# Eighteen loads of one input move from SyncE's DMA queue to ScalarE's, every engine keeping its order

## The chip, the cores and the metric

The kernel runs on one core of one Trainium2 chip. The metric is the device time of one execution in microseconds. Before the change it was 199.9 us, the median of three runs (199.68 to 200.76). About half a per cent, 1.0 us here, is what a measurement of this kernel can tell from no change.

## The reference, cut to what matters

Two stages. The first is a recurrence over 768 time steps for 4 batches and 8 heads with head size 40; its output, laid out as 4 x 768 x 320, is the input `x` of the second, a mixer over tokens and channels.

```python
for t in range(S):                                    # per batch and head, state is 40 x 40
    y[t]  = r[t] @ state
    Sa    = state @ a[t]
    state = state * w[t][:, None] - outer(Sa, b[t]) + outer(v[t], k[t])
...
theta = x @ w_theta
zr, zi = x * cos(theta), x * sin(theta)
u = x + w_tok_r @ zr + w_tok_i @ zi                   # over the 768 tokens
out = u + max(u @ w_ch, 0)
```

All inputs and the output are 32-bit floats.

## The kernel before, in words

The 768 steps of each of the 4 batches are cut into 6 chunks of 128, so there are 24 tiles, numbered 0 to 23, each with 128 steps in the partitions and 8 heads x 40 values in a row. Within a tile the recurrence is written as matrix products, so a tile is a long chain over all engines. A tile's decay factors come first: ScalarE takes the logarithm of `w` (tile `lw`), TensorE sums it over time, ScalarE takes exponentials (`ex`, and `we` for the sum without the step itself). GpSimd then multiplies: `kb` is `k` or `b` by `ex`, and `ah` is `a` by `we` (function `product`, line 456, the only reader of the input `a`; `DVE` does it for tiles 0 and 1). TensorE transposes `ah` (lines 404 and 408), ScalarE or VectorE copies the transposed piece out of PSUM as `aT`, and TensorE multiplies `aT` with the transposed `kb` into score matrices (line 603), which VectorE or ScalarE masks (lines 612 and 614). More products follow for the state and the read-out. Once the six tiles of a batch are read out, its mixer stage (the products of line 910 on TensorE, sines on ScalarE, products with `x` on GpSimd) is worked in between the tiles of the next batch; that of the last batch ends the kernel.

The order of all the work is written out by hand. Each step is recorded as an `Op` by `add`, with its engine and with what it reads and writes; `Plan.order` then emits the steps in the order of the list `ORDER`, a permutation of 1602 numbers. An engine executes its own instructions strictly in that order, and waits at each for what it needs. The list `HOMES` gives each result its PSUM bank, `PICK` names the steps that go to their second engine.

Every input load of the recurrence is issued by SyncE, whose work in the kernel is issuing DMAs and waiting to be allowed to: `loads(i)` records for tile `i` the loads of `w`, `k`, `b`, `a` and from tile 8 on `v` (line 436), and for every second tile two loads of `r` (and of the early `v`) for two tiles at once (line 448). A load of 160 KB goes in rows of 40 floats, 160 bytes each. Its buffer is one of a ring: 5 buffers for `a` (`raw_a`, named `raw_a_68` to `raw_a_72` in the built program), 4 each for `w` and for `k` with `b` (`raw_kb`). A load may be issued once the buffer's last reader is done. Besides, the DMAs of SyncE and ScalarE share eight semaphores in turn, so each waits until the DMA eight places earlier in `ORDER` has landed. GpSimd issues the loads of the mixer's weights (lines 961 and 989), and SyncE the stores of the result and, late in the program, eleven DMA transposes. ScalarE issues one DMA, half of the last store (line 938).

Of the kernel before, what the change touches and what calls it, by code (L numbers as in the profile page):

```python
# [19 lines left out]
FROM_POOL = 4  # L20
EXCLUSIVE = 7
# [198 lines left out]
def kernel(  # L220
# [14 lines left out]
    nc = tc.nc  # L235
# [19 lines left out]
    raw_a = sb("raw_a", [128, H, D], FP32, NA)  # L255
# [820 lines left out]
```

## Time and profile before

| | |
|---|---|
| median of the runs | 199.9 us (199.68 to 200.76) |
| span of the profiled execution, first to last instruction | 195.9 us |
| time of the profiled execution itself | not among the three, so the median stands for it: 4.0 us lie outside the span |
| TensorE matmuls busy | 184.3 us, 94% |
| VectorE busy | 163.3 us, 83% |
| ScalarE busy | 150.6 us, 77% |
| GpSimd busy | 145.1 us, 74% |
| queue of SyncE's DMAs | 29.19 MB, packets for 76.6% of 16 engines' span |
| queue of GpSimd's DMAs | 2.97 MB, 9.3% |
| queue of ScalarE's DMAs | 0.08 MB, 0.1% |

In the profile's lines `PE` is TensorE's matmuls, `PEld` its weight loads, `DVE` VectorE, `ACT` ScalarE, `POOL` GpSimd. `SPq` and `ACTq` are the instruction sequencers of SyncE and ScalarE: waiting for semaphores and issuing DMAs, during which the arithmetic unit of ScalarE is not counted as busy. `L456` is line 456 of the kernel. A DMA has three times: its issue begins, the issue takes a while on the sequencer, and the data land later.

### The profile page before, as it was taken

The page shows a single profiled execution, that of the slowest core. Times are in us where ns is not written, and L with a number is a line of the kernel's source. Part 1 is how long each engine was busy: PE and PEld are TensorE (multiplying, and loading weights), DVE is VectorE, ACT ScalarE, POOL GpSimd, SP SyncE. Part 2 cuts the span into 40 slices and gives each one's busy share as a digit, 9 for nine tenths or more (in the row PEclk, how much of TensorE's full clock was granted, in tenths as well). Part 3 has the DMA queues.
Part 4 walks back from the last instruction along what each step waited for, and adds up shares of the span by engine and source line. Part 5 has one row for each costly group of instructions (what it writes and reads, how often), then busy time and mean ns, then how long its engine had stood idle before and what let it go on. Part 6 is the DMA issues. An engine that isn't in the chain of part 4 may idle for free.

```text
span 195.9 us, 8473 instructions
## 1 busy us (share of the span) xinstructions
PE 184.3 (94%) x3516; PEld 145.4 (74%) x3516; DVE 163.3 (83%) x260; ACT 150.6 (77%) x336; POOL 145.1 (74%) x211
## 2 busy tenths in 40 slices
PE   7889899999997999999899999999999999999992
PEld 6767687887786778887577787887788768767661
DVE  5378799999998999898897999999999938664453
ACT  3575879799997997999689599979999867575111
POOL 8367466579969999696699959868879997469100
PEclk9999999999999999999999999999999999999998
DMA  5999897999999999979999997789899977535055
GB/s 118 217 205 182 148 214 157 174 171 206 216 183 166 197 180 185 225 122 200 179 183 158 166 200 129 164 147 180 161 178 203 168 172 102 128 136 74 32 197 172
DMA packets 134646, 32.78 MB, mean 167 GB/s; under 512 B 124816, under 2 KB 134608, under 8 KB 134608
## 3 DMA queue, kind: packets, MB, share of 16 engines
q1 hardware_dynamic: 131680, 29.19, 76.6%
q0 software_dynamic: 2784, 2.97, 9.3%
q8 instruction: 27, 0.44, 0.9%
q10 hardware_dynamic: 144, 0.08, 0.1%
q14 instruction: 11, 0.09, 0.1%
HBM read 29.54 MB, written 3.93 MB: 171 GB/s over the span
## 4 chain that ended last, share of the span: by engine, by line
PE 61%; DMA 12%; POOL 9%; ACT 6%; DVE 4%; SPq 4%; issue 2%; ACTq 0%; DVEq 0%; POOLq 0%
PE banks L910 16%; PE banks L603 9%; PE banks L404 8%; PE banks L792 5%; DMA raw_a<-in_a_dram 4%; DMA raw_kb<-in_k_dram 4%; SPq L436 3%; PE banks L408 3%; DMA uT<-up 2%; PE banks L569 2%; PE banks L663 2%; POOL kb L456 2%; PE banks L686 2%; PE banks L802 2%; DMA raw_v<-in_v_dram 2%
## 5 line engine op out<-in xcount | busy, mean ns | idle before, releaser
L456 POOL TENSOR_TENSOR kb<-raw_kb,ex 128x320 bf16<-128x320 f32 x46 | 37.1, 814 | 8.0 <-DMA raw_kb<-in_k_dram 3.0
L910 PE MATMUL banks<-zr,wtok_r 128*128 128x320 bf16 x144 | 41.0, 300 | 0.2
L910 PE MATMUL banks<-zi,wtok_i 128*128 128x320 bf16 x144 | 40.8, 299 | 0.1
L456 POOL TENSOR_TENSOR ah<-raw_a,we 128x320 bf16<-128x320 f32 x22 | 19.0, 865 | 12.9 <-ACT we L506 4.7
L612 DVE TENSOR_TENSOR lamu<-banks,mask_p 128x1024 bf16<-128x1024 f32 x22 | 26.8, 1219 | 1.5 <-PE banks L603 0.8
L612 DVE TENSOR_TENSOR psi<-banks,mask_p 128x1024 bf16<-128x1024 f32 x22 | 26.8, 1219 | 0.8 <-PE banks L603 0.7
L612 DVE TENSOR_TENSOR phi<-banks,mask_n 128x1024 bf16<-128x1024 f32 x18 | 21.9, 1216 | 1.6 <-POOL r L462 1.3
L612 DVE TENSOR_TENSOR lamv<-banks,mask_p 128x1024 bf16<-128x1024 f32 x17 | 20.7, 1219 | 1.6 <-PE banks L603 1.0
L894 POOL TENSOR_TENSOR zi<-cs,xp 128x320 bf16<-128x320 f32 x22 | 17.2, 791 | 2.0 <-ACT cs L879 1.2
L910 PEld LDWEIGHTS <-wtok_r 128*128 128x128 bf16 x144 | 14.0, 97 | 5.6 <-issue 0.3
L603 PE MATMUL banks<-aT,kbT 64*128 64x128 bf16 x384 | 17.2, 217 | 0.9 <-DVE kbT L426 0.3
L894 POOL TENSOR_TENSOR zr<-cs,xp 128x320 bf16<-128x320 f32 x22 | 17.4, 802 | 0.1
L910 PEld LDWEIGHTS <-wtok_i 128*128 128x128 bf16 x144 | 14.0, 98 | 3.8 <-issue 0.3
L829 PE MATMUL banks<-kb,lamv 128*128 128x40 bf16 x192 | 14.9, 180 | 0.0
L831 PE MATMUL banks<-kb,lamu 128*128 128x40 bf16 x192 | 14.8, 179 | 0.0
L603 PEld LDWEIGHTS <-kbT 64*128 64x128 bf16 x384 | 11.8, 94 | 3.7 <-ACT kbT L422 1.1
L829 PEld LDWEIGHTS <-lamv 128*128 128x128 bf16 x192 | 13.2, 96 | 0.4
L916 DVE TENSOR_TENSOR up<-banks,xp 128x320 bf16<-128x320 f32 x22 | 10.6, 485 | 3.1 <-PE banks L910 2.9
L831 PEld LDWEIGHTS <-lamu 128*128 128x128 bf16 x192 | 13.0, 96 | 0.0
L472 ACT ACTIVATE lw<-raw_w 128x320 bf16<-128x320 f32 x24 | 11.5, 477 | 1.5 <-DMA raw_w<-in_w_dram 1.3
L496 ACT ACTIVATE ex<-banks 128x328 f32<-128x328 f32 (+1 forms) x24 | 10.8, 450 | 2.2 <-PE banks L491 1.1
L822 PE MATMUL banks<-gd,rT 128*128 128x80 bf16 x80 | 12.2, 197 | 0.0
(202 smaller groups left out, 583.0 us busy)
## 6 DMA issues: line engine op xcount, KB each, us to landing
raw_w<-in_w_dram SPq DMA_DIRECT2D x24, 160.0 KB, 4.3
raw_v<-in_v_dram SPq DMA_DIRECT2D x24, 160.0 KB, 3.7
raw_a<-in_a_dram SPq DMA_DIRECT2D x24, 160.0 KB, 3.9
raw_kb<-in_k_dram SPq DMA_DIRECT2D x24, 160.0 KB, 4.2
raw_kb<-in_b_dram SPq DMA_DIRECT2D x24, 160.0 KB, 4.2
raw_r<-in_r_dram SPq DMA_DIRECT2D x24, 160.0 KB, 3.8
out_dram<-oo SPq DMA_DIRECT2D x9, 160.0 KB, 2.6
wrow_i<-in_moe_w_tok_i_dram POOLq DMA_DIRECT2D x6, 192.0 KB, 5.3
```

The source lines that it names most:

```text
L404: nc.tensor.transpose(out=t[:, m * 128:m * 128 + 128], in_=src, identity=ident)
L456: pool = ("POOL", lambda: nc.gpsimd.tensor_tensor(out=dst, in0=in0, in1=in1, op=ALU.mult))
L472: add("ACT", "ln", i, lambda: nc.scalar.activation(out=paired(lw)[:, :, :, 0:D], in_=paired(raw_w[s4]), func=AF.Ln), 473, [("raw_w", s4)], ...
L496: got = add("ACT", "exp", i, lambda: nc.scalar.activation(out=ex[:, :, 0:D] if no_total else ex.rearrange("p h x -> p (h x)"), in_=sums(ps ...
L603: nc.tensor.matmul(t[:, q, g, :], lhsT=lhs[g][rows(q)], rhs=rhs[g][rows(q)], start=True, stop=True)
L612: add("DVE", kindm, i, lambda: nc.vector.tensor_tensor(out=flat, in0=whole(), in1=mask.to_broadcast([128, 2 * G, 128]), op=ALU.mult), 1217 ...
L822: nc.tensor.matmul(t[:, g * 80:g * 80 + 80], lhsT=by_two(rT)[g], rhs=gd[:, 2 * g:2 * g + 2, :], start=True, stop=False, skip_group_check=True)
L829: nc.tensor.matmul(o, lhsT=lamv[:, p, g, :], rhs=kb[:, 0, h, 0:D], start=first, stop=False, skip_group_check=True)
L831: nc.tensor.matmul(o, lhsT=lamu[:, p, g, :], rhs=kb[:, 1, h, 0:D], start=False, stop=True, skip_group_check=True)
L894: pool = ("POOL", lambda: nc.gpsimd.tensor_tensor(out=dst, in0=in0, in1=in1, op=ALU.mult))
L910: nc.tensor.matmul(acc(), lhsT=wtok[nm][j][:, s], rhs=zs[c][:, s], start=n == 0 and c == 0, stop=n == NT - 1 and c == 1)
L916: add("DVE", "uadd", q, lambda: nc.vector.tensor_tensor(out=u, in0=acc(), in1=x, op=ALU.add), 488, [pk, x_key(q)], [u_key(q)], at="row")
```

## The change

The loads of `a` of tiles 6 to 23, eighteen of them, are recorded for ScalarE and issued with `nc.scalar.dma_start` in place of `nc.sync.dma_start`. Nothing else is loaded, computed or stored in another way, and the buffers are the same. `ORDER` is written anew: a moved load stands behind the ScalarE instruction that was running when SyncE issued that load in the kernel before, and the other instructions stand on every engine as they stood.

```diff
+SECOND = 6
...
 ORDER = [
-    0, 7, 3, 6, 1, 20, 2, 21, 8, 23, 24, 4, 27, 32, 9, 30, 22, 33, 31, 25, 5, 34, 26, 12, 28,
+    0, 7, 3, 6, 1, 20, 2, 21, 23, 8, 24, 27, 30, 4, 32, 31, 9, 22, 33, 5, 25, 12, 26, 34, 69,
...
     def loads(i):
         for key, dst, src in load(i):
-            add("SP", "l" + key[0][4:], i,
-                lambda dst=dst, src=src: nc.sync.dma_start(out=dst, in_=src),
-                600, [], [key], work=1030)
+            other = key[0] == "raw_a" and i >= SECOND
+            add("ACT" if other else "SP", "l" + key[0][4:], i,
+                lambda dst=dst, src=src, q=nc.scalar if other else nc.sync: q.dma_start(
+                    out=dst, in_=src), 600, [], [key], work=1030)
```

In the changed file the lines below the new constant have a number that is one higher, and those below the load two higher.

SyncE's program about the load of `a` for tile 13, some 86 us into the profiled execution; `raw_v_77` and the like are buffers of the inputs that follow the letter.

```order
L436 DMA raw_v_77<-in_v_dram 128x8x40
L448 DMA raw_r_80<-in_r_dram 128x1x320
L436 DMA raw_a_71<-in_a_dram 128x8x40
L436 DMA raw_v_78<-in_v_dram 128x8x40
L436 DMA raw_kb_75<-in_k_dram 128x8x40
```

The same place of SyncE's program after the change.

```order
L438 DMA raw_v_77<-in_v_dram 128x8x40
L450 DMA raw_r_80<-in_r_dram 128x1x320
L438 DMA raw_v_78<-in_v_dram 128x8x40
L438 DMA raw_kb_75<-in_k_dram 128x8x40
L438 DMA raw_kb_75<-in_b_dram 128x8x40
```

The load has left the row, and the load of `v` moves up behind that of `r`. ScalarE's program at the same time, before: `gd` is the state for the read-out, `aT` the transposed `ah`, `we` the exponential that `ah` needs, `psi` a score matrix.

```order
L718 CAST gd_209<-banks 128x320
L718 CAST gd_208<-banks 128x320
L422 COPY aT_184<-banks 128x256
L514 ACTIVATE we_179<-sx_183 128x320
L614 ACTIVATE psi_198<-banks 128x1024
```

The same place of ScalarE's program after the change.

```order
L720 CAST gd_209<-banks 128x320
L720 CAST gd_208<-banks 128x320
L423 COPY aT_184<-banks 128x256
L438 DMA raw_a_71<-in_a_dram 128x8x40
L516 ACTIVATE we_179<-sx_183 128x320
```

The load now stands between two computing instructions, ahead of the exponential `we`, and everything behind it on ScalarE comes one place later.

188 rows, old and new, of the table ORDER are left out of this document.

## The prediction

> **What bounds the kernel now.** I read the page first: busy shares, the slices, and the chain of work that ended last.
>
> ```profile
> span 195.9 us, 8473 instructions
> PE 184.3 (94%) x3516; PEld 145.4 (74%) x3516; DVE 163.3 (83%) x260; ACT 150.6 (77%) x336; POOL 145.1 (74%) x211
> DMA  5999897999999999979999997789899977535055
> PE 61%; DMA 12%; POOL 9%; ACT 6%; DVE 4%; SPq 4%; issue 2%; ACTq 0%; DVEq 0%; POOLq 0%
> ```
>
> TensorE's matmuls are busy for 94% of the span and are 61% of the chain. So a microsecond saved elsewhere counts only where TensorE stood still for it, and one lost counts only where TensorE then stands still. The DMA digits are at 9 nearly all the way to the last fifth: the transfers run close to what is moved at all, but they are 12% of the chain, not the bound. Next I asked where the chain passes through a load.
>
> ```profile
> 45.14 0.38 POOL wrow_i L989
> ...
> 48.22 7.07 DMA raw_kb<-in_k_dram
> 55.36 0.58 POOL kb L456
> ...
> 86.11 8.33 DMA raw_a<-in_a_dram
> 94.58 0.88 POOL ah L456
> ```
>
> Two loads in the steady part land late, at 55 us a load of `k` and at 94 us a load of `a`, each while GpSimd's own loads are under way (the first row is one of their issues). Then the list of waits, for what that lateness costs.
>
> ```profile
> POOL ah L456 <- DMA raw_a<-in_a_dram: 3.4, 1, 3.4
> ...
> POOL kb L456 <- DMA raw_kb<-in_k_dram: 3.0, 2, 1.8
> ...
> PEld L408 <- POOL ah L456: 1.4, 2, 1.1
> ```
>
> GpSimd waits 3.4 us once for `a`, but TensorE waits for `ah` only 1.4 us in two places together (total, times, longest). This 1.4 us is the most that earlier loads of `a` and `k` can be worth at these two places. The rest of GpSimd's waiting never reaches TensorE.
>
> Then ScalarE, which takes over the issues, in stretches of 20 us (stretch, length, busy us and instructions, TensorE's granted clock, DMA share, GB/s).
>
> ```profile
> 20.00:40.00 20.00, 16.72 (x44) 1.00 0.89 175
> 40.00:60.00 20.00, 18.70 (x45) 1.00 1.04 192
> 60.00:80.00 20.00, 18.00 (x41) 1.00 1.04 183
> 80.00:100.00 20.00, 17.58 (x36) 1.00 1.00 175
> 100.00:120.00 20.00, 16.74 (x39) 1.00 0.93 170
> 120.00:140.00 20.00, 18.38 (x44) 1.00 0.89 166
> 140.00:160.00 20.00, 18.92 (x41) 1.00 0.93 181
> ```
>
> It is idle 3.28, 1.30, 2.00, 2.42, 3.26, 1.62 and 1.08 us in them. That is the room for new work, and it is small in three of the seven.
>
> **The change, part by part.** What it removes: eighteen issues from SyncE. The row of the tile and SyncE's timeline say how long such an issue takes (start, length).
>
> ```profile
> L436 SPq DMA_DIRECT2D raw_a<-in_a_dram x24: 575/630/1815, 2.0 to 148.2; - x24
> ...
> DMA to landing us min/median/max: 3.0/3.9/8.7
> ```
>
> ```profile
> 40.04 1.81 SPq L436 DMA_DIRECT2D raw_a<-in_a_dram  x1
> 41.95 0.69 SPq L436 DMA_DIRECT2D raw_kb<-in_k_dram  x1
> ...
> 51.27 0.66 SPq L436 DMA_DIRECT2D raw_a<-in_a_dram  x1
> ...
> 56.34 0.63 SPq L436 DMA_DIRECT2D raw_a<-in_a_dram  x1
> 65.00 0.58 SPq L436 DMA_DIRECT2D raw_a<-in_a_dram  x1
> 69.63 0.61 SPq L436 DMA_DIRECT2D raw_a<-in_a_dram  x1
> 74.01 0.68 SPq L436 DMA_DIRECT2D raw_a<-in_a_dram  x1
> ...
> 87.43 3.02 SPq L436 DMA_DIRECT2D raw_kb<-in_k_dram  x1
> ...
> 121.03 0.63 SPq L436 DMA_DIRECT2D raw_a<-in_a_dram  x1
> 125.02 0.58 SPq L436 DMA_DIRECT2D raw_a<-in_a_dram  x1
> 132.06 1.67 SPq L436 DMA_DIRECT2D raw_a<-in_a_dram  x1
> 139.70 0.58 SPq L436 DMA_DIRECT2D raw_a<-in_a_dram  x1
> 142.85 1.40 SPq L436 DMA_DIRECT2D raw_a<-in_a_dram  x1
> 148.18 1.60 SPq L436 DMA_DIRECT2D raw_a<-in_a_dram  x1
> ```
>
> The rows of `raw_a` are twelve of the eighteen, those of the four stretches with at most 2.00 us of room; the other six fall into the roomy ones. SyncE issues without a pause: the load at 40.04 ends at 41.85 and the next begins at 41.95. So 18 x 0.63 = 11 us leave SyncE, and each later load can be issued sooner by what has gone before it. The moved load of 40.04 stands ahead of the late `k` of 48.22, and 1.81 us of issuing go with it, as much as its consumer waited (1.8). The late `a` of 86.11 is itself moved, and no longer shares a queue with what SyncE issued before it.
>
> The gain is thus between 0 and 1.4 us. I take 0.5, nearer to nothing, for two reasons. A wait of TensorE that goes uncovers the next one, and the same transfers still have to share the DMA engines. The Trainium skill, page DMA: Bandwidth & Descriptors, section Issuing engines are not separate DMA queues, holds that the queues end on the same 16 engines and that a second issuer saves only the issuing time; by that the gain at 94 us, where the issue took 0.59 us of 8.33, would be next to nothing.
>
> What it adds: eighteen issues on ScalarE. The trace has one DMA issue there, at the very end, with its twin on SyncE.
>
> ```profile
> L938 ACTq EVENT_SEMAPHORE  x1: 38/38/38, 191.1 to 191.1; - x1
> ...
> L938 ACTq DMA_DIRECT2D out_dram<-wrow_r x1: 371/371/371, 192.1 to 192.1; - x1
> L938 SPq DMA_DIRECT2D out_dram<-wrow_r x1: 332/332/332, 192.4 to 192.4; - x1
> ```
>
> ```profile
> 190.99 0.54 ACT L422 COPY uT<-banks 128x192 f32<-128x192 f32 x2 [1.49 <-PE banks L404]
> ```
>
> For the same half store ScalarE takes 371 ns against 332, so a load that takes SyncE 0.575 us unhindered should take ScalarE 0.575 x 371/332 = 0.64 us, an estimate. How much of it stops the arithmetic? The semaphore instruction ahead of that store ran at 191.1, while the two copies from 190.99 to 191.53 were still at work: the sequencer runs ahead of the arithmetic unit. An issue can then lie under the instruction before it. A typical one is
>
> ```profile
> L496 ACT ACTIVATE ex<-banks 128x328 f32<-128x328 f32 (+1 forms) x24 | 10.8, 450 | 2.2 <-PE banks L491 1.1
> ```
>
> 0.45 us long. One bound: of each issue 0.64 - 0.45 = 0.19 us shows, 4 x 0.19 = 0.76 us at most in a stretch (120 to 140), under the 1.62 us of room, so the cost is 0. The other: the whole 0.64 us stands on ScalarE. Then 40 to 60 needs 1.92 for 1.30 of room (0.62 over), 60 to 80 needs 1.92 for 2.00, 120 to 140 needs 2.56 for 1.62 (0.94 over), 140 to 160 needs 1.28 for 1.08 (0.20 over), and the rest fits: 1.8 us. I take 0.6, a third of the way, because the one row that shows the order of things (191.1 inside 190.99 to 191.53) is on the side of the overlap. If the cover is gone, because ScalarE had just waited and its sequencer has no lead, the price of one issue is its whole 0.64 us, and it falls on whatever stands behind it: in the place shown above, `we` and then `psi`, for which GpSimd and TensorE wait.
>
> The added issues also wait, each for the DMA eight places earlier in the order, on a semaphore that the two queues share, and on ScalarE such a wait holds all its arithmetic. Eight issues of 0.63 us are 5.0 us; a load lands 3.9 us after its issue in the median, at most 8.7. Landings that late come where issues are slow too (the issue of 3.02 us at 87.43 is of that time), so I cost this at nothing; one miss would cost 8.7 - 5.0 = 3.7 us at most.
>
> The sum: 199.9 - 0.5 + 0.6 = 200.0 us. It is made in the span of 195.9 us and carried over to the median, with the 4.0 us outside the span left as they are.
>
> **The rivals.**
>
> Slower, ScalarE stalls as SyncE does. In SyncE's rows the same issue takes 0.58 us or up to 1.81 us, although SyncE's next issue follows at once in both cases: something downstream pushes back. If it pushes on whoever issues, ScalarE inherits these lengths in its tightest stretches. 40 to 60 then needs 3.10 us for 1.30, 120 to 140 needs 3.46 for 1.62, 140 to 160 needs 3.00 for 1.08, and 60 to 80 fits with 1.87: 1.80 + 1.84 + 1.92 = 5.6 us. With 0.45 us of each hidden, 0.45 + 0.04 + 1.02 = 1.5 us. So 201.4 to 205.5, the middle 203.5 us. It decides once a moved issue takes over about a microsecond. For it: four of the twelve rows are that long. Against it: ScalarE's queue would be nearly empty at each issue, and an own queue need not push back. The Trainium skill, same page, section Queues, rings and completion order, says that SyncE and ScalarE have a row of rings each, but no descriptor generator of their own; by that rule the push-back would be shared and this rival would hold. No row of this profile shows both queues loaded at once.
>
> Slower, nothing is hidden and nothing gained: the whole 0.64 us stands on ScalarE, and TensorE's 1.4 us stay. 199.9 + 1.8 = 201.7 us. For it: ScalarE often starts just after a wait; against it: the row at 191.1.
>
> Faster, a second queue carries more. If the transfers of two queues overlap better than those of one, the loads land earlier and both stops of TensorE go, with the issue hidden: 199.9 - 1.4 = 198.5 us. For it: in the stretches with GpSimd's loads in flight beside SyncE's the DMA share is 1.04, elsewhere 0.89 to 0.93, so two queues together are busier than one. Against it: TensorE has only these 1.4 us to give, and the stretches differ in more than their queues.
>
> That the change does not do what it says I rule out: the orders above show the load gone from one row and present in the other.
>
> **How the numbers follow.** Forecast, 200.0 us (its own range 199.2 to 200.9): 0.45. ScalarE stalls like SyncE, 203.5: 0.20. Nothing hidden and nothing gained, 201.7: 0.15. Faster, 198.5: 0.20. With about half a per cent, 1.0 us, as what can be told from no change: faster 0.20, same 0.45, slower 0.35. The range goes from 198.4, which takes in the faster rival, to 203.6, which takes in the unhidden issue and the lower half of the stalled one; that leaves out half of 0.20 above and some 0.05 below.
>
> **What would show it right or wrong.** Right: ScalarE's issue rows for `raw_a` are near 0.64 us, ScalarE's busy time stays near 150.6 us, TensorE's wait for `ah` is below 1.4 us, and no new wait of TensorE or GpSimd for ScalarE's `we`, `kbT` or `aT` adds up to more than a microsecond. The stalled rival shows in issue rows on ScalarE over 1 us, with ScalarE idle behind them. The faster one shows in landing times of `raw_a` well below 3.9 us and no wait for `ah`. I am wrong if the time is under 199 or over 201, and most plainly if ScalarE's sequencer stands in front of a load waiting for another load to land.

## The result, and the profile after

The changed kernel takes 214.99 us (median of four runs, 214.8 to 215.37), the kernel before 200.33 us beside it: 1.078 times as long, 95% interval 1.073 to 1.084. That is 14.7 us more, where 200.0 us with a range up to 203.6 us was forecast.

The page of the changed kernel, in the rows that answer to those of before:

```profile
span 213.4 us, 8469 instructions
PE 190.5 (89%) x3516; PEld 150.2 (70%) x3516; DVE 163.3 (76%) x260; ACT 151.5 (71%) x336; POOL 145.4 (68%) x211
PE 51%; DMA 7%; ACT 6%; DVE 6%; SPq 4%; POOL 3%; issue 2%; ACTq 1%; POOLq 0%; DVEq 0%
```

The span is 17.5 us longer, the medians differ by 14.7. Nearly all of the gap between the two comes from the profiled execution before, which was a quick one: in the changed kernel 1.7 us lie outside the span (215.14 us against 213.4), so that execution took some 197.6 us, an estimate from 195.9 + 1.7, less than its median; the 4.0 us outside the span, with the median standing for it, were too much. TensorE stands idle for 213.4 - 190.5 = 22.9 us where it was 195.9 - 184.3 = 11.6 us, and it is busy 6.2 us longer with the same 3516 products. ScalarE's busy time has hardly grown (151.5 against 150.6 us). So ScalarE did not get more work; something stops.

The row of the moved loads, and how long they take to land:

```profile
L438 ACTq DMA_DIRECT2D raw_a<-in_a_dram x18: 374/375/444, 44.5 to 165.7; - x18
...
DMA to landing us min/median/max: 2.5/3.9/7.9
```

An issue takes ScalarE 0.375 us, 0.444 at the longest, and the data land after 3.9 us as before. Neither the issue nor the transfer has become slow, nor does a slow issue on SyncE lengthen one on ScalarE that falls into it:

```profile
46.69 1.59 SPq L450 DMA_DIRECT2D raw_r<-in_r_dram  x1
47.88 0.37 ACTq L438 DMA_DIRECT2D raw_a<-in_a_dram  x1
```

But the first moved load, which SyncE issued at 40.04 us, is issued at 44.5. The list of waits (engine and line, what it waited for, total us, times, longest):

```profile
PE banks L665 <- ACT nx L658: 6.4, 2, 5.9
ACT nx L658 <- DMA raw_kb<-in_b_dram: 6.3, 1, 6.3
...
ACT rT L588 <- DMA raw_w<-in_w_dram: 2.9, 1, 2.9
```

ScalarE waits 6.3 us for a load of `b` in front of `nx`, an instruction that reads a PSUM bank and no input at all, and 2.9 us for a load of `w` in front of `rT`, a copy out of PSUM. ScalarE's timeline shows what stands between (start, length; what the idle time before it ended with):

```profile
38.23 0.47 ACT L474 ACTIVATE lw<-raw_w 128x320 bf16<-128x320 f32 x1
44.53 0.44 ACTq L438 DMA_DIRECT2D raw_a<-in_a_dram  x1
45.01 0.43 ACT L658 CAST nx<-banks 128x320 bf16<-128x320 f32 x1 [6.31 <-DMA raw_kb<-in_b_dram]
...
60.52 0.47 ACT L658 CAST nx<-banks 128x320 bf16<-128x320 f32 x1
63.38 0.43 ACTq L438 DMA_DIRECT2D raw_a<-in_a_dram  x1
63.91 0.65 ACT L588 COPY rT<-banks 128x256 f32<-128x256 f32 x2 [2.92 <-DMA raw_w<-in_w_dram]
```

Each time it is a moved load. ScalarE was done with `lw` at 38.70 and issued the load of `a` for tile 6 only at 44.53, 5.83 us later; done with `nx` at 60.99, it issued that for tile 8 at 63.38, 2.4 us later. In the kernel before no load stood at the first of these places:

```profile
38.26 0.47 ACT L472 ACTIVATE lw<-raw_w 128x320 bf16<-128x320 f32 x1
39.03 0.42 ACT L656 CAST nx<-banks 128x320 bf16<-128x320 f32 x1 [0.30 <-PE banks L650]
```

Two more moved loads stand in the same way for 1.5 us (issued at 47.88) and 2.0 us (136.82): 11.7 us in the four. The other fourteen did not hold up the arithmetic. SyncE's timeline has what the first two waited for:

```profile
40.56 1.67 SPq L438 DMA_DIRECT2D raw_kb<-in_b_dram  x1
...
55.03 2.16 SPq L438 DMA_DIRECT2D raw_w<-in_w_dram  x1
```

The load of `b` issued at 40.56 landed at 44.51, and ScalarE's issue follows at 44.53; the load of `w` issued at 55.03 landed at 63.36, and ScalarE's issue follows at 63.38. Neither load has anything to do with `a`. The two shorter stops end in the same way, with the landing of a load of `r` at 47.86 and of one of `v` at 136.74. TensorE stops with ScalarE:

```profile
45.49 0.42 PE L665 MATMUL banks<-nx,phi 128*128 128x40 bf16 x8 [5.91 <-ACT nx L658]
...
64.95 0.61 PE L405 MATMUL banks<-wide,nu 128*128 128x128 bf16 x4 [2.99 <-ACT nu L669]
```

Why ScalarE waits for these loads is in the program as it was built. The DMAs of SyncE and ScalarE share eight completion semaphores, and each DMA waits until the one before it on the same semaphore has landed. The description of the kernel before says that this is the DMA eight places earlier in `ORDER`. That holds where SyncE alone issues; with two issuers it does not. The semaphores are handed out in turn in the order in which the framework's builder places the instructions, and it places SyncE's loads far ahead of ScalarE's work. The load of `a` for tile 6 is DMA number 42 of the list, counted from 0, but number 52 of the built program; its semaphore was last given to number 44, the load of `b` for tile 7, which stands in the list behind it. The Trainium skill, page DMA: Bandwidth & Descriptors, section Why a DMA increments its semaphore by 16 and not by 1, says why such a wait is there at all: two DMAs in flight on one semaphore can fill its count together before the first has landed. The trace agrees that the wait is for the whole landing: both issues above begin 0.02 us after it.

### The profile page after: what moved, and what is told of

Same layout as the page of the kernel before. It is cut to its first block, busy times and chain, and to the rows that moved or that the text cites. A ratio compares the mean times of both kernels' runs of the same rounds, so it can differ in the third digit from the quotient of the medians.

```text
span 213.4 us, 8469 instructions
## 1 busy us (share of the span) xinstructions
PE 190.5 (89%) x3516; PEld 150.2 (70%) x3516; DVE 163.3 (76%) x260; ACT 151.5 (71%) x336; POOL 145.4 (68%) x211
## 4 chain that ended last, share of the span: by engine, by line
PE 51%; DMA 7%; ACT 6%; DVE 6%; SPq 4%; POOL 3%; issue 2%; ACTq 1%; POOLq 0%; DVEq 0%
PE banks L912 14%; PE banks L605 8%; PE banks L405 7%; PE banks L794 5%; DMA raw_w<-in_w_dram 4%; SPq L438 3%; PE banks L409 2%; PE banks L804 2%; DMA raw_v<-in_v_dram 2%; DMA raw_r<-in_r_dram 2%; PE banks L688 2%; PE banks L665 2%; PE banks L833 1%; SPq L450 1%; PE banks L831 1%
## 5 line engine op out<-in xcount | busy, mean ns | idle before, releaser
L605 PE MATMUL banks<-aT,kbT 64*128 64x128 bf16 x384 | 17.8, 223 | 1.4 <-ACT kbT L423 0.5
L831 PE MATMUL banks<-kb,lamv 128*128 128x40 bf16 x192 | 15.4, 183 | 0.0
L833 PE MATMUL banks<-kb,lamu 128*128 128x40 bf16 x192 | 15.3, 181 | 0.0
L665 PE MATMUL banks<-nx,phi 128*128 128x40 bf16 x192 | 9.0, 182 | 6.8 <-ACT nx L658 6.4
L511 DVE TENSOR_TENSOR sx<-banks,lw 128x320 f32<-128x320 f32 x17 | 8.2, 484 | 8.3 <-ACT ex L498 8.2
L658 ACT CAST nx<-banks 128x320 bf16<-128x320 f32 x20 | 8.6, 430 | 7.8 <-DMA raw_kb<-in_b_dram 6.3
L831 PEld LDWEIGHTS <-lamv 128*128 128x128 bf16 x192 | 13.7, 97 | 0.3
L833 PEld LDWEIGHTS <-lamu 128*128 128x128 bf16 x192 | 13.5, 99 | 0.0
```

What stands on the lines that cost most here:

```text
L605: nc.tensor.matmul(t[:, q, g, :], lhsT=lhs[g][rows(q)], rhs=rhs[g][rows(q)], start=True, stop=True)
L658: add("ACT", "nx", i, lambda: nc.scalar.copy(out=nx, in_=ps(pk)[:, 0:DM]), 426, [pk], [("nx", s2)], alts=(("DVE", lambda: nc.vector.tensor ...
L665: nc.tensor.matmul(t[:, h * D:h * D + D], lhsT=phi[:, h % 2, h // 2, :], rhs=nx[:, h * D:h * D + D], start=False, stop=True, skip_group_ch ...
L831: nc.tensor.matmul(o, lhsT=lamv[:, p, g, :], rhs=kb[:, 0, h, 0:D], start=first, stop=False, skip_group_check=True)
L833: nc.tensor.matmul(o, lhsT=lamu[:, p, g, :], rhs=kb[:, 1, h, 0:D], start=False, stop=True, skip_group_check=True)
```

## The experiments

In the kernels below `ORDER` is broken into lines in another way, so that a line has a number up to five lower than in the changed kernel.

**The order alone.** All loads back on SyncE (`SECOND` is empty), everything else as changed.

```diff
-            other = key[0] == "raw_a" and i >= SECOND
+            other = key[0] == "raw_a" and i in SECOND
```

> The order of after, but all loads of `a` back on SyncE. Theory (ScalarE stands in front of a moved load until the DMA before it on the same semaphore has landed): no load on ScalarE, so no such wait, 199.5 to 201.0 us like before. Rival (the rewritten order costs something by itself, wherever the load is issued): stays well above before, up to 215 us. Rival (the issue on ScalarE, or its second queue, costs the time): also 199.5 to 201.0, so this run speaks only against the order.

Measured: 199.88 us, 0.999 of before (0.994 to 1.004). No cost of the rewritten order is to be seen.

**One load alone.** The same line with `SECOND = (6,)`.

> Only the load of tile 6 stays on ScalarE, the other seventeen go back to SyncE. By the built program it follows on its semaphore a load of `r` that lands at 46.6 us in the trace of before, and ScalarE is there at 38.7. Theory (wait on the shared semaphore): one stop of 6 to 8 us on ScalarE, and a loss of 4 to 9 us: 204 to 209 us, TensorE's granted clock below 0.9 in the stretch from 40 to 60 us. Rival (the issue or the second queue costs the time, 14.7 us over eighteen loads, 0.8 us each): 200.5 to 201.5 us.

Measured: 205.68 us, 1.032 of before (1.027 to 1.037), 6.4 us. One issue of 0.5 us cannot cost that; ScalarE's timeline has the stop:

```profile
38.43 0.47 ACT L469 ACTIVATE lw<-raw_w 128x320 bf16<-128x320 f32 x1
47.32 0.50 ACTq L433 DMA_DIRECT2D raw_a<-in_a_dram  x1
47.86 0.43 ACT L653 CAST nx<-banks 128x320 bf16<-128x320 f32 x1 [8.96 <-DMA raw_r<-in_r_dram]
```

With another set of loads on ScalarE the semaphore is another one, and so is the DMA that is waited for: now a load of `r`. The stop is 47.32 - 38.90 = 8.4 us, longer than any in the changed kernel.

**The waits alone.** All loads on SyncE; ScalarE issues nothing, but its instruction behind thirteen of the places waits for the landing for which the moved load waited; at the other five that was the landing of another moved load, and the wait is left out. `WAITS` names the pairs. `ORDER` lists the loads waited for earlier than in the changed kernel, ahead of the instruction that waits; on every engine the trace has the same work in the same order as with the order alone.

```diff
+            at = len(nc.cur_bb.bb.instructions)
             o.fn()
+            first = nc.cur_bb.bb.instructions[at]
+            if o.idx in WAITS.values():
+                landed[o.idx] = first.name
+            if o.idx in WAITS:
+                tc.add_manual_dep(first, landed[WAITS[o.idx]], mybir.DependencyInfo(
+                    mybir.DependencyClass.Sync, mybir.DependencyReason.DATA), reason="wait")
```

> All loads on SyncE, and nothing is issued on ScalarE; but at thirteen of the eighteen places ScalarE's next instruction waits until the DMA has landed for which the moved load waits in after (at the other five the moved load waits for another moved load, which is left out). Theory (ScalarE's wait makes the loss, not the issue): 211 to 219 us, with ScalarE's stops where after has them and TensorE's granted clock below 0.9 between 40 and 80 us. Rival (the issue or the second queue costs the time): 200 to 203 us, since no queue is changed.

Measured: 215.98 us, 1.080 of before (1.071 to 1.088), the loss of the change with no load moved. The stop stands where the changed kernel has it:

```profile
38.39 0.47 ACT L471 ACTIVATE lw<-raw_w 128x320 bf16<-128x320 f32 x1
46.78 0.43 ACT L655 CAST nx<-banks 128x320 bf16<-128x320 f32 x1 [7.92 <-DMA raw_kb<-in_b_dram]
```

**The loads on ScalarE without the waits.** All eighteen stay on ScalarE. So that the builder hands out the semaphores in the order of the list, SyncE's next load behind each moved one waits for the ScalarE instruction ahead of it.

```diff
+    last = tie = None
...
-            o.fn()
+            done = o.fn()
+            if o.kind == "la" and o.eng == "ACT":
+                tie = last
+            elif o.eng == "ACT" and done is not None:
+                last = done
+            elif o.eng == "SP" and tie is not None:
+                tc.add_manual_dep(done.ins, tie.ins.name, mybir.DependencyInfo(
+                    mybir.DependencyClass.Sync, mybir.DependencyReason.DATA), reason="in step")
+                tie = None
```

> All eighteen loads stay on ScalarE at the places of after; SyncE's next load behind each now waits for the ScalarE instruction ahead of the moved load, which by the trace of before has ended by then. With it the builder hands out the eight semaphores in the order of the list, and each moved load follows on its semaphore a DMA that had landed 0.5 to 4.9 us before the issue in the trace of before. Theory (the wait on the shared semaphore makes the loss): 199.3 to 201.5 us, ScalarE's issues still near 0.37 us each and none of the stops of 2 to 6 us ahead of them. Rival (the issues on ScalarE or the second queue cost the time): stays at 210 to 215 us, since eighteen loads are issued there as before.

Measured: 197.25 us, 0.991 of before (0.988 to 0.994). The eighteen issues are there, as short as in the changed kernel, and the loss is not; it has even turned into a gain of 1.8 us. The row of the issues, and the first of them in ScalarE's timeline:

```profile
L433 ACTq DMA_DIRECT2D raw_a<-in_a_dram x18: 374/375/431, 37.6 to 147.0; - x18
```

```profile
37.62 0.37 ACT L418 COPY v<-banks 128x256 f32<-128x256 f32 x1 [0.44 <-PE banks L400]
37.63 0.43 ACTq L433 DMA_DIRECT2D raw_a<-in_a_dram  x1
37.89 0.47 ACT L469 ACTIVATE lw<-raw_w 128x320 bf16<-128x320 f32 x1
```

The issue of 0.43 us begins while the copy of `v` is at work and ends after `lw` has begun: the sequencer issues a load that stands behind `lw` while the arithmetic unit still has `v` and `lw` to do, and nothing waits. The four runs together settle the cause of the loss: with the waits and without the moved loads it is there, with the moved loads and without the waits it is not, and the order alone is free.

**Whose the gain is.** The waits of SyncE are kept for the loads of the same eighteen tiles (`TIED` is 6), with all loads on SyncE (`SECOND` is 24). The edit is against the kernel in step.

```diff
-            if o.kind == "la" and o.eng == "ACT":
+            if o.kind == "la" and o.i >= TIED:
```

> All loads on SyncE, with the eighteen waits of e2_in_step kept: SyncE's next load behind each load of `a` waits for the ScalarE instruction that ran ahead of it. The question is whose the gain of e2_in_step is (0.991 of before). If it comes from the second queue and from SyncE's relief: no gain here, 0.995 to 1.005 of before, and GpSimd again waits about 3 us for `a` near 94 us. If it comes from pacing SyncE's loads: 0.988 to 0.995.

Measured: 200.52 us, 1.007 of before (1.003 to 1.011). Neither of the two expectations: the waits on SyncE cost about 1.5 us, and with them in place the moved loads are worth 1.007 - 0.991 = 1.6% of the time, some 3 us. The gain is not the pacing's.

**A looser step.** SyncE waits for the last ScalarE instruction but one (`last` is now a list of them). It was to show whether these 1.5 us come from SyncE's starting late.

```diff
-                tie = last
+                tie = last[-2]
```

> The kernel of e2_in_step with each of SyncE's eighteen waits for the last ScalarE instruction but one in place of the last. The semaphores then still follow the list closely: by the trace of before the DMA that a moved load waits for has landed before ScalarE gets there at sixteen places, 0.16 us before it at a seventeenth, and 0.2 us after it at one (tile 14). e5_ties_alone showed that the waits on SyncE cost 0.8 per cent by themselves. If that is because SyncE's next load starts late: 0.983 to 0.990 of before. If the pace of SyncE does not matter once `a` has left its queue: 0.988 to 0.995 like e2_in_step. If ScalarE meets a semaphore too early again: over 1.0, with the stop in ScalarE's row.

> The kernel of e2_in_step once more, beside the looser one on the same chip. If its gain is the kernel's and not that chip's: 0.988 to 0.995 of before, as in the first run (0.991).

Measured on one chip: the looser one 198.47 us, 0.995 of before (0.991 to 0.999); the stricter one again 197.6 us, 0.989 (0.984 to 0.995). The gain of the stricter one repeats, on another chip. The looser one gains no more, so SyncE's later start is not shown to be what its waits cost. No moved load holds the arithmetic in it: one, issued at 97.30, had to wait for a landing at 97.28, but the copy ahead of it was at work until 97.40.

**Twice the issues.** The kernel in step, with each moved load cut into two of four heads each, behind each other.

```diff
+            def both(dst=dst, src=src):
+                nc.scalar.dma_start(out=dst[:, 0:4], in_=src[:, 0:4])
+                return nc.scalar.dma_start(out=dst[:, 4:8], in_=src[:, 4:8])
```

> The kernel of e2_in_step with each of the eighteen loads issued as two loads of four heads each, both on ScalarE: the same bytes, in the same rows of 160 bytes, with eighteen more issues of about 0.37 us, 6.7 us in all. If ScalarE's issues lie under other work: within 0.5 us of e2_in_step, 0.988 to 0.995 of before. If a third of each shows, as I took it for the prediction: 2.2 us more, 0.999 to 1.005. If the whole issue shows: up to 6.7 us more, 1.02 to 1.03.

Measured: 201.79 us, 1.014 of before (1.008 to 1.019), 4.5 us above the kernel in step. The first and the second halves have rows of their own:

```profile
L433 ACTq DMA_DIRECT2D raw_a<-in_a_dram x18: 374/375/512, 38.2 to 152.8; - x18
L434 ACTq DMA_DIRECT2D raw_a<-in_a_dram x18: 465/520/1590, 38.8 to 153.2; - x18
```

```profile
123.87 0.59 ACT L422 COPY kbT<-banks 128x512 f32<-128x512 f32 x1
123.90 0.37 ACTq L433 DMA_DIRECT2D raw_a<-in_a_dram  x1
124.31 0.52 ACTq L434 DMA_DIRECT2D raw_a<-in_a_dram  x1
124.93 0.44 ACT L496 ACTIVATE ex<-banks 128x328 f32<-128x328 f32 x1 [0.47 <-PE banks L603]
```

The first issue lies under `kbT`, which works until 124.46. The second, 0.52 us long, ends at 124.83, and `ex` begins behind it after 0.47 us of nothing: the cover of one instruction is used up by the first. The row puts this pause down to products of line 603 (600 in the kernel in step), but there `ex` begins while the same products are still to run, without a pause:

```profile
120.00 0.44 ACT L493 ACTIVATE ex<-banks 128x328 f32<-128x328 f32 x1
...
120.14 0.40 PE L600 MATMUL banks<-aT,kbT 64*128 64x128 bf16 x8
```

But the whole is not only this; the list of waits has GpSimd waiting longer for the halves of `a`:

```profile
POOL ah L456 <- DMA raw_a<-in_a_dram: 6.8, 3, 4.4
```

The run does not part the two, so no price of a second issue in the total follows.

**TensorE's clock.** I had a second theory for the 6.2 us by which TensorE's busy time grew: a stop costs twice, by its length and by the lower clock behind it. In windows of 3 us (length, PE, PEld, DVE, ACT and POOL busy us with instructions, TensorE's granted clock, DMA share, GB/s) the changed kernel reads:

```profile
44.00:47.00 3.00, 1.51 (x34) 1.38 (x34) 0.68 (x2) 1.37 (x4) 0.00 (x0) 0.50 0.92 218
47.00:50.00 3.00, 2.21 (x27) 1.94 (x24) 1.43 (x2) 1.70 (x5) 0.79 (x2) 0.50 1.21 210
50.00:53.00 3.00, 3.00 (x33) 2.36 (x32) 2.55 (x3) 1.72 (x6) 3.00 (x6) 0.50 1.30 211
...
65.00:68.00 3.00, 3.00 (x42) 2.69 (x43) 1.77 (x3) 2.08 (x4) 0.34 (x1) 0.50 1.12 215
```

Behind the stops of 5.91 and 2.99 us the granted clock is 0.50. The Trainium skill, page TensorE: Matmul & The Clock Gate, section Part 1: The HAM clock gate, puts the fall to half speed after an idle window of about 3.4 us; here a stop of 2.99 us was enough, and one of 2.10 us that ended at 139.06 (0.51 from 139 to 142 us). To hold the clock, TensorE works in the three longest stops on products of the constant `busy`, which nothing reads (batches added at three instructions; 44, 21 and 14 products in a first run, and, since one took 57 ns and they filled only half of the stops, the 92, 48 and 32 below in a second).

```diff
-WARM = {21: (0, 25), 30: (1, 4), 33: (2, 1), 28: (1, 8), 41: (1, 11)}
+WARM = {21: (0, 25), 30: (1, 4), 33: (2, 1), 28: (1, 8), 41: (1, 11), 329: (5, 92), 532: (5, 48), 1046: (0, 32)}
```

> The kernel of after, all its waits unchanged, but TensorE works through its three longest stops (5.9, 3.0 and 2.1 us) on 79 products of a constant that nothing reads: 44, 21 and 14 of them, each batch shorter than its stop. Theory (the stops cost twice: their own length, 11 us, and a lower granted clock behind them, which lengthens TensorE's busy time by 6 us): the granted clock stays above 0.95 from 40 to 80 us, and the time falls by 2 to 6 us, to 209 to 213 us. Rival (the lower clock costs nothing that is not hidden): 214 to 216 us, at whatever clock.

> e7_clock_held again with longer batches, since its products took 57 ns each and covered only half of the stops: 92, 48 and 32 of them, 5.2, 2.7 and 1.8 us. The granted clock should now stay above 0.95 from 40 to 60 us. If the lower clock behind the stops is a part of the loss: 205 to 212 us. If the loss is set by the landings for which ScalarE waits, and a faster TensorE only waits longer for them: 213 to 216 us, with ScalarE's stops longer than in after by about what TensorE saves.

Measured: 215.46 us (1.078, 1.070 to 1.085) with the short batches, 216.43 us (1.091, 1.081 to 1.101) with the long ones, and a mean granted clock of 0.974 and 0.990 where the changed kernel has 0.952. In the traces the clock stands at 0.50 for 20.5 us of the changed kernel, 10.2 us with the short batches and 3.4 us with the long ones (the last microseconds left out). So the short batches held it only in part; the long ones held it through the three stops, and nothing was gained. What became of the faster products is seen in a window of the second run and in TensorE's timeline:

```profile
44.00:47.00 3.00, 2.82 (x65) 2.60 (x62) 0.76 (x2) 1.37 (x4) 0.00 (x0) 1.00 0.88 198
47.00:50.00 3.00, 0.51 (x10) 0.39 (x8) 1.27 (x2) 0.70 (x3) 0.00 (x0) 1.00 1.01 195
```

```profile
40.11 5.30 PE L1035 MATMUL banks<-busy 128*128 128x128 bf16 x92 [0.30 <-DVE lamv L609]
45.58 0.35 PE L660 MATMUL banks<-nx,phi 128*128 128x40 bf16 x8 [0.18 <-ACT nx L653]
...
49.79 0.38 PE L400 MATMUL banks<-wide,xp 128*128 128x128 bf16 x4 [2.49 <-ACT nu L664]
```

TensorE is done sooner at full clock and then waits 2.49 us for `nu`, which stands behind the second moved load on ScalarE; that load waits for a landing at 48.79 us, no earlier than in the changed kernel (47.86). All stops of ScalarE ahead of moved loads add up to 14.6 us here, against 11.7 in the changed kernel. The batches themselves held up little: the first product behind the longest begins at 45.58, against 45.49. My second theory falls: the products ran slowly in time that ScalarE's waits had set anyway. TensorE's 6.2 us of longer busy time are a consequence; nothing of them came back in time when the clock was held.

## Why the prediction was wrong, step by step

- **The step that failed** is the one that priced the added waits: "Eight issues of 0.63 us are 5.0 us; a load lands 3.9 us after its issue in the median", "so I cost this at nothing; one miss would cost 8.7 - 5.0 = 3.7 us at most". It took the DMA eight places earlier in the list for the one that is waited for, and so a DMA issued 5 us before. The built program decides, and there the DMA ahead on the semaphore was issued by SyncE 40.56 - 38.70 = 1.9 us *after* ScalarE had finished `lw` ahead of the load for tile 6, and its 3.95 us to the landing came on top. That stop of 5.83 us alone is more than the step's worst case, and there were four, 11.7 us together, for a term put at nothing. The prediction named the sign by which it would be seen to be wrong, ScalarE's sequencer in front of a load waiting for another to land, and took the risk for small without reading the semaphores.
- **Room on ScalarE and the issue's length.** I scaled SyncE's 0.575 us by the two stores' 371/332 to 0.64 us and took 0.6 us for eighteen of them. An issue took 0.375 us, like the store, and lay under the instruction before it. The scale was wrong in kind: SyncE's 0.575 us is what an issue takes that follows another at once. In the changed kernel five of SyncE's loads have a pause of at least 1 us ahead of them, and these take it 0.367 or 0.368 us each; the 87 of line 438 with less than 0.25 us ahead take 0.73 in the median. With the waits gone, eighteen of them show no loss. The overlap that I read from the one semaphore row at 191.1 us was there; the price was mis-sized by all of it.
- **The stalled rival** (ScalarE inherits SyncE's issues of up to 1.81 us) is refuted for single loads by 374/375/444. The row that the prediction missed, with both queues at issuing, is there now: eight of the eighteen meet an issue of over 1 us on SyncE, as at 47.88, and none takes over 0.444 us. The slower outcome came by another mechanism. Where a second load follows at once, an issue of 1.59 us is seen on ScalarE too. The Trainium skill, page DMA: Bandwidth & Descriptors, section Queues, rings and completion order, gives SyncE and ScalarE rows of rings but no descriptor generator of their own; the single issues show nothing of a push-back by the other queue, and whether the doubled ones do is open.
- **What leaves SyncE.** I took a gain of 0.5 us, and 1.4 at most, from two waits of TensorE. With the waits out of the way the kernel in step gains 1.8 and 2.1 us in its two measurements (0.991 and 0.989 of 199.4), although SyncE pays for it. The case nearest to this is the faster rival's, 198.5 us. Whether the bound was too low is not shown, since 1.4 us lies inside both intervals, but it was read from one execution: in the profile of the order alone, with the same work in the same order, TensorE's weight loads wait for `ah` 1.9 us, not 1.4. With SyncE's waits in place the move is worth some 3 us, twice the bound. Where this comes from is open: in the second profile of the kernel in step (197.6 us) GpSimd still waits 3.6 us in all for `a`, and yet the time is as good.
- **TensorE as the bound** held as it was put: what was lost is what TensorE stood still for, 11.3 us more, and what it did slowly meanwhile.

## What to carry to other kernels

Before a DMA is moved into the queue of an engine that also computes, read in the built program which DMA stands ahead of it on its completion semaphore: the wait is for that one's landing, it may belong to another queue and to later data, and it holds every instruction behind it. On SyncE, which computes nothing here, such a wait holds up other issues alone; on ScalarE four of them, 11.7 us together, came with a loss of 14.7 us, and a slow clock behind a stop need not add to the price. If the two engines are kept in step, here by a wait on the issuing engine's side, the same move gained 0.9 to 1.1%.

## What the runs showed of the hardware that was not expected

- In the changed kernel the length of an issue goes with whether another stands right before it in the same queue, and not with the engine: a 160 KB load behind a pause takes 0.375 us on ScalarE and 0.37 us on SyncE (five loads). Back to back SyncE takes 0.63 us for `a` in the median (before the change), and ScalarE 0.52 us (465/520/1590) for the second half of a load directly behind the first.
- ScalarE's sequencer issues a DMA while up to two earlier computing instructions are still to be finished (37.63 inside 37.62 to 37.99, with `lw` behind), so a single issue need not cost its arithmetic anything.
- TensorE's granted clock fell to 0.50 behind a stop of 2.99 us and to 0.51 behind one of 2.10 us, and with the clock held through the stops the time did not fall (1.091 against 1.078 of before).
